# Scaling of an mLSTM chunk's values cut in halves and moved, with four small moves around it, in a fused mLSTM and MLP kernel

## The chip, the cores and the metric

The kernel runs on one core of one Trainium2 chip, in one launch. The metric is the device time of a whole execution in microseconds (us). The kernel before was run five times: 469.13, 469.29, 468.72, 469.12 and 468.61 us, median 469.12. All runs had a granted TensorE clock of 1.0 of full speed.

The engines are named as the profile names them: PE is TensorE (matmuls), PEld its weight loads, DVE is VectorE, ACT is ScalarE, POOL is GpSimd and SP is SyncE, which here does nothing but issue DMAs.

## The reference

The first half is an mLSTM cell with B=4 batches, H=8 heads, S=768 tokens and head size D=40, the second an MLP with a quick GELU on the 3072 tokens x 320 values that the cell gives.

```python
for t in range(S):
    m_new = np.maximum(f_gate[:, :, t] + m, i_gate[:, :, t])
    f_stab = np.exp(f_gate[:, :, t] + m - m_new)
    i_stab = np.exp(i_gate[:, :, t] - m_new)
    m = m_new
    C = f_stab[..., None, None] * C + i_stab[..., None, None] * einsum('bhd,bhe->bhde', v_t, k_t)
    n = f_stab[..., None] * n + i_stab[..., None] * k_t
    h_tilde = einsum('bhde,bhe->bhd', C, q_t)
    denom = np.maximum(np.abs(einsum('bhd,bhd->bh', n, q_t)), 1.0)
    y[:, :, t] = sigmoid(o_t) * h_tilde / denom
x = y.transpose(0, 2, 1, 3).reshape(3072, 320)
h = x @ w_in                                   # 320 x 2048
out = (h * sigmoid(1.702 * h)) @ w_out         # 2048 x 320
```

The inputs of the cell are float32. `moe_w_in` and `moe_w_out` are float64 in memory, and the kernel reads them as pairs of 32-bit words.

## The kernel before, in words

**Tiling.** The 768 tokens are cut into NW=6 chunks w of 128. In each chunk the recurrence is worked out as a masked matrix product within the chunk (scores, weights, values) plus what the state of the chunks before gives. The 32 pairs of batch and head go by batch b (8 heads) in chunk 0, and by halves c (16 heads, two batches) in later chunks. Then the chunk's 512 tokens (4 batches x 128) go through the MLP in 8 pairs of 128 hidden columns (`up`, later `up_fast`, which saves multiplications by Strassen's scheme) and through `w_out` (`down`, `down_fast`). While PE works at the MLP of chunk w, the cell of chunk w+1 is done in between.

**Converting the weights.** The float64 words are turned into float32 in 20 pieces of 128 x 512. Pieces 0 to 9 are `w_in`: 0, 1, 3, 4, 5, 6, 8, 9 go into `w_in_sb` (two halves c of the first 256 rows, by 512 columns), 2 and 7 into `w_in_x` (the last 64 rows). Pieces 10 to 19 are `w_out`. Each piece takes six instructions:

```python
242  A.activation(out=dst, in_=hi.bitcast(FP), func=AF.Abs)              # convert_high
246  A.activation(out=lo, in_=lo, func=AF.Copy, scale=2.0 ** -29)        # convert_low
255  V.tensor_scalar(out=dst, in0=dst, scalar1=HI_MIN, scalar2=HI_MAX, op0=OP.max, op1=OP.min)
256  V.tensor_scalar(out=dst_u, in0=dst_u, scalar1=3, ...)               # convert_mid, as 255 and 258
258  V.scalar_tensor_tensor(out=dst_u, in0=hi, scalar=0xC0000000, ...)
264  V.tensor_tensor(out=dst_u, in0=dst_u, in1=lo, op=OP.add)            # convert_add
```

The first two are on ScalarE, the others on VectorE. Where the profile names a piece by its target, piece 0 is `w_in_sb` at L264 before 26 us, piece 1 the next `w_in_sb`, piece 2 the first `w_in_x`.

**What sets the order.** The schedule is manual: each engine runs its instructions in the order in which the program issues them, and waits by semaphores for the other engines' results. So a call's place in the program is its place on each engine's queue. Tiles come from pools with a fixed number of buffers; PSUM has two pairs of banks (`ps_a`, tag "a": `p_t`, `p_cols`, `p_x`, `p_o`, `p_i`, `p_c`, `p_s` in turn) and four single banks (`ps_m`). A tile that takes a buffer waits until the readers of its last tenant are done. Nearly all DMAs are issued by SP, one after the other; each chunk's gates go out to DRAM and come back as columns and rows: `m_row` (L298), `st_row` and `d_row` (L322) are written by `gates`, `columns_in` (L340 to 347) reads `raw` back, and `spread` (L391 to 398) reads `m_row` into `wt`, spread over the partitions. In the program `spread(1)` stands at j=4 of chunk 0, behind `load(1, "v")` and `columns_in(1)`.

**The start and chunk 0** (L821 to 864). PE begins with 18 matmuls of 128 columns on a tile of zeros (L197) that no one reads. Then, per batch b, come the transposes of k and q (L371), the weights of the chunk (`weights`, L411 to 426: matmuls into PSUM and two exponentials on ScalarE), the scores (L436 to 445), and for b of 2 and 3 the values of batch b-2 (`values`, L478 to 489) with `outputs` (L458 to 476). `outputs` forms `y` on VectorE and, in chunk 0, ends with a tail copy of 64 columns on GpSimd (L476). `seam` (L520) transposes a batch's `y` into `xT`, the MLP's input: three transposes, the third of which reads the tail copy, and copies out of PSUM on ScalarE, but for the last batch, whose first copy is on VectorE (L528). Between the third and the fourth seam stand `columns(0)` (L354: one transpose `p_cols` and one Exp that turn the gates' sums into `cols`), the first half of the conversion of piece 1, and `keep_busy(1, spare, 7)` (L189 to 193), one matmul of 512 and seven of 32 columns that nobody reads. Pieces 1 and 2 are converted behind the last seam.

**The MLP of chunk 0** (L880 to 900). For even j, `up` does two pairs of columns: L608 multiplies `w_in_sb`, L614 `w_in_x`. The pieces of weights that later j need are converted ahead of and inside these calls (`converted`, L866): pieces 3 and 4 ahead of the first `up`, piece 5 inside it. In the same loop `scale(0, 0)`, `carry(0, 0)`, `scale(0, 1)`, `carry(0, 1)` follow `up` at j = 0, 1, 2, 3. `scale` (L570 to 574) is one GpSimd instruction that multiplies 16 heads of `v_st` (128 partitions x 656 values) by an exponential in `cols`, into `vw`; `carry` (L576) multiplies `k` by `vw` on PE and copies the sum into the state. GpSimd needs nothing from PE for both scalings, so it runs them one behind the other.

```python
891  (carry if j % 2 else scale)(0, j // 2)       # for j < B
```

Later, `weights(1, 0)` has ScalarE do 32 exponentials on `wt` (L429) when the rows are there and GpSimd the mask (L433), `scores(1, c)` multiplies them with the scores on VectorE (L456), and `values(1, 0)` multiplies `wt` with `v_st` into `p_o` (L497) and the queries with the state into `p_i` (L505). Pieces 17 to 19 are converted during `down` (L934).

Of the kernel before, what the change touches and what calls it, by code (L numbers as in the profile page):

```python
# [8 lines left out]
FP = mybir.dt.float32  # L9
# [3 lines left out]
OP = mybir.AluOpType  # L13
# [4 lines left out]
L = 128  # L18
# [8 lines left out]
def kernel(  # L27
# [13 lines left out]
    B, H, S, D = q.shape  # L41
    BH = B * H
    DM = H * D
# [4 lines left out]
    D1 = D + 1  # L48
# [5 lines left out]
    PH = 2 * H  # L54
# [3 lines left out]
    const = ctx.enter_context(tc.tile_pool(name="const", bufs=1))  # L58
# [134 lines left out]
            T.matmul(bank[:, 0:32], idle, idle[:, 0:32], start=True, stop=True)  # L193

    p_idle = ps_m.tile([128, W], FP, tag="m", name="p_idle")
    for _ in range(18):
        T.matmul(p_idle[:, 0:128], idle, idle, start=True, stop=True)  # L197
    ident = const.tile([128, 128], FP, name="ident")
    make_identity(nc, ident)
    make_identity(nc, ident_b)  # L200
# [17 lines left out]
    for t in (k_0, q_st):  # L218
        G.memset(t[:, :, D:DP], 0.0)

    state = [const.tile([128, BH // 2, D1], FP, name=f"state{i}") for i in range(2)]
    state_mid = const.tile([128, BH // 2, D1], FP, name="state_mid")

# [20 lines left out]
    def convert_low(n):  # L244
        lo, hi, dst = words(n)
        A.activation(out=lo, in_=lo, func=AF.Copy, scale=2.0 ** -29)
# [211 lines left out]
    def outputs(w, hs, u):  # L458

        n = hs.stop - hs.start  # L460
        c, b = divmod(hs.start // H, 2)
        den = work.tile([L, n, 1], FP, tag="den", name="den")
        V.tensor_scalar(out=den, in0=u[:, :, D:D1], scalar1=-1.0, scalar2=1.0, op0=OP.mult, op1=OP.max)
        V.tensor_tensor(out=den, in0=u[:, :, D:D1], in1=den, op=OP.max)
        V.reciprocal(out=den, in_=den)
        z = eo[w][:, hs, :]
        V.scalar_tensor_tensor(out=z, in0=z, scalar=1.0, in1=u[:, :, 0:D], op0=OP.add, op1=OP.mult)
        if b == 0:
            ys[w, c] = work.tile([L, 2, DM + 64], FP, tag="y", name="y")
        for x in range(n // H):  # L470
            y, h = ys[w, c][:, b + x], slice(hs.start + x * H, hs.start + x * H + H)
            V.scalar_tensor_tensor(out=y[:, 0:DM].rearrange("p (h d) -> p h d", d=D), in0=eo[w][:, h, :], scalar=0.5,
                                   in1=den[:, x * H:(x + 1) * H].to_broadcast([L, H, D]), op0=OP.mult, op1=OP.mult)
        if w == 0:
            y = ys[w, c][:, b:b + n // H]
            G.tensor_copy(out=y[:, :, DM:DM + 64], in_=y[:, :, DM - 64:DM])  # L476

    def values(w, c):  # L478
        if w == 0:
            hs = slice(c * H, (c + 1) * H)  # L480
            po = ps_m.tile([L, H, D1], FP, tag="m", name="p_o")
            for p in range(NP):
                for i in range(2):
                    h = 2 * p + i
                    for x in range(2):
                        t = slice(x * HL, x * HL + HL)
                        T.matmul(po[t, h, :], wt[w, c][:, p, i, t], v_st[:, c * H + h, :], start=True, stop=True)  # L487
            outputs(w, hs, po)
            return
        hs = slice(c * PH, (c + 1) * PH)  # L490
        po, pi = banks("p_o"), banks("p_i")

        for j in range(NJ):
            for i in range(2):
                for x in range(2):
                    t, r = slice(x * HL, x * HL + HL), slot(i, x)
                    T.matmul(po[t, i, j * D1:(j + 1) * D1], wt[w, c][r, j, i, :], v_st[r, c * PH + 2 * j + i, :],  # L497
                             start=True, stop=True)
        for j in range(NJ):
            b, p = 2 * c + j // NP, j % NP  # L500
            for i in range(2):
                r = slice(i * 64, i * 64 + D)
                for x, s in enumerate((state[w % 2], state_mid)):
                    t = slice(x * HL, x * HL + HL)
                    T.matmul(pi[t, i, j * D1:(j + 1) * D1], qT[w, b][r, p, t], s[r, c * NJ + j, :], start=True,  # L505
                             stop=True)
        u = work.tile([L, PH, D1], FP, tag="u", name="u")
        v = u.rearrange("s (j i) d -> s i j d", i=2)
        g = cols[w][:, BH + c * PH:BH + (c + 1) * PH].rearrange("s (j i) -> s i j", i=2).unsqueeze(3)
        view = lambda z: z[:, :, 0:NJ * D1].rearrange("s i (j d) -> s i j d", d=D1)  # L510
        V.tensor_tensor(out=v, in0=view(pi), in1=g.to_broadcast([L, 2, NJ, D1]), op=OP.mult)
        V.tensor_tensor(out=v, in0=view(po), in1=v, op=OP.add)
        outputs(w, hs, u)

    def x_of(w):
# [51 lines left out]
        engine.tensor_tensor(out=dst[:, js], in0=old[:, js], in1=d.unsqueeze(2).to_broadcast([128, NJ, D1]),  # L567
                             op=OP.mult)

    def scale(w, c):  # L570
        hs = slice(c * PH, (c + 1) * PH)
        vw[w, c] = work.tile([L, PH, D1], FP, tag="u", name="vw")
        e = cols[w][:, 2 * BH + c * PH:2 * BH + (c + 1) * PH].unsqueeze(2).to_broadcast([L, PH, D1])
        G.tensor_tensor(out=vw[w, c], in0=v_st[:, hs, :], in1=e, op=OP.mult)  # L574

    def carry(w, c):  # L576
        js = slice(c * NJ, (c + 1) * NJ)
# [255 lines left out]
    for b in range(B):  # L833
        if b >= 2:
            transposes(0, b)
            open_first(b - 2)
            values(0, b - 2)
        weights(0, b)
        if b == 0:
            convert_high(0)  # L840
            transposes(0, 1)
        scores(0, b)
        if b == 0:
            convert_mid(0)
        if b == 1:
            convert_low(0)
            convert_add(0)
    load_gates(1)
# [5 lines left out]
    values(0, 3)  # L854
    seam(0, 0, 1)
    seam(0, 1, 0)
    columns(0)
    convert_high(1)
    spare = ps_m.tile([128, W], FP, tag="m", name="p_idle")
    keep_busy(1, spare, 7)  # L860
    seam(0, 1, 1)
    convert_low(1)
    convert_end(1)
# [16 lines left out]
    for w in range(NW):  # L880
        more = w + 1 < NW
        if w == 0:
            for j in range(NF // 2):
                if j % 2 == 0:
                    ahead, behind = converted[j // 2]
                    run([(convert, p) for p in ahead] + [(fetch, p) for p in fetched.get(j // 2, ())])
                    up(w, j, lambda: run([(convert, p) for p in behind]))
                if j == 6:
                    load(1, "o")
                if j < B:  # L890
                    (carry if j % 2 else scale)(0, j // 2)
                if j == 3:
                    masks()
                    gates(1)
                if j == 4:
                    load(1, "v")
                    columns_in(1)
                    spread(1)
                if j >= B:
                    transposes(1, j - B)  # L900
        else:
            token_sums(w)
            if more:
                gates(w + 1)
                load(w + 1, "o")
            for j in range(NF // 2):
                up_fast(w, j)
                if w == 1 and j < 4:
                    weight_sums(j)
                if more and j == 2:  # L910
                    load(w + 1, "vk")
                    columns_in(w + 1)
                    spread(w + 1)
                if more and j:
                    for n in ((), (0, 2), (4,), (6, 1), (3,), (5, 7), ())[j - 1]:
                        block_transposes(w + 1, n)
                if more and j == 7:
                    columns_turn(w + 1)
                if 2 <= j < 6:
                    hidden_difference(w, j - 2)  # L920
                if j >= 6:
                    hidden_sums(w, (j - 6,), G)
            gelu_fast(w, NF // 2 - 1)
            hidden_sums(w, (2, 3), V)
        side = attention(w + 1) if more else {}
        if w == 0:
            columns_turn(1)

            blocks = [(lambda b=b, n=n: down(w, b, n)) for n0 in (0, 2) for b in range(B) for n in (n0, n0 + 1)]
        else:  # L930
            blocks = down_fast(w, 0) + down_fast(w, 1)
        for i, block in enumerate(blocks):
            if w == 0 and i in (0, 4, 5):
                convert((17, 18, 19)[max(i - 3, 0)])  # L934
            if w + 2 < NW and i == (6 if w == 0 else 0):
                load_gates(w + 2)
            if w + 2 < NW and i == 13:
                load_squares(w + 2, "kq" if w else "k")
            if w == 0 and i == 15:
                load_squares(w + 2, "q")  # L940
            block()
            run(side.get(i, []))
            if w == 0 and i in (11, 13):
                input_sums(slice(0, 4) if i == 11 else slice(4, 8))
# [30 lines left out]
```

## Time and profile before

| | |
|---|---|
| median of five runs | 469.12 us |
| the profiled execution's own time | 469.13 us |
| its span in the profile | 467.4 us |
| PE busy | 462.1 us, 99% of the span, 5063 matmuls |
| PEld busy | 388.2 us, 83% |
| DVE busy | 341.9 us, 73% |
| ACT busy | 189.7 us, 41% |
| POOL busy | 156.8 us, 34% |
| DMA traffic | 52.21 MB, a mean of 112 GB/s |

By stage, from the table of windows (DMA is the share of the 16 DMA engines):

| stretch, us | what PE does | length | PE busy | DMA |
|---|---|---|---|---|
| 0 to 26 | chunk 0 of the cell | 26 | 24.55 | 0.93 |
| 26 to 33 | last seam, first `up` | 7 | 6.17 | 1.07 |
| 33 to 70 | `up` of chunk 0 | 37 | 37.00 | 0.97 |
| 70 to 94.4 | `down`, cell of chunk 1 | 24.4 | 24.40 | 0.55 |
| 94.4 to 116 | `down`, cell of chunk 1 | 21.6 | 21.60 | 0.55 |
| 116 to 467 | chunks 1 to 5 | 351 | 348.41 | 0.51 |

How to read it: the profile is one execution, recorded on the chip; its own time (469.13) is 1.7 us longer than the span between the first and the last recorded instruction. A line of the timeline gives the start, the duration, the engine, the program line, the operation with output and inputs, the sizes and a count of instructions that stand together; a bracket at the end is the idle time of that engine just before, with the engine, tile and line that ended it. SPq lines are DMA issues on SP's queue. Busy time on PE is the time that matmuls are in it; the table says where PE waits (stretches whose busy time is less than their length), not whether a matmul could be shorter.

### The profile page before, as it was taken

The page shows a single profiled execution, that of the slowest core. Times are in us where ns is not written, and L with a number is a line of the kernel's source. Part 1 is how long each engine was busy: PE and PEld are TensorE (multiplying, and loading weights), DVE is VectorE, ACT ScalarE, POOL GpSimd, SP SyncE. Part 2 cuts the span into 40 slices and gives each one's busy share as a digit, 9 for nine tenths or more (in the row PEclk, how much of TensorE's full clock was granted, in tenths as well). Part 3 has the DMA queues.
Part 4 walks back from the last instruction along what each step waited for, and adds up shares of the span by engine and source line. Part 5 has one row for each costly group of instructions (what it writes and reads, how often), then busy time and mean ns, then how long its engine had stood idle before and what let it go on. Part 6 is the DMA issues. An engine that isn't in the chain of part 4 may idle for free.

```text
span 467.4 us, 12343 instructions
## 1 busy us (share of the span) xinstructions
PE 462.1 (99%) x5063; PEld 388.2 (83%) x5063; DVE 341.9 (73%) x698; ACT 189.7 (41%) x431; POOL 156.8 (34%) x142
## 2 busy tenths in 40 slices
PE   8999999999999999999999999999999999999997
PEld 6867777777778999678999767999878999876997
DVE  5787998789788976688875778887768866544612
ACT  5676776500536700554800453900454820264100
POOL 5020004300798700266700257610158620157100
PEclk9999999999999999999999999999999999999999
DMA  8999979228994025999024998115999305000000
GB/s 164 194 272 166 292 134 219 30 54 193 181 146 111 3 72 132 192 125 162 6 60 111 196 148 149 23 36 122 177 140 124 88 18 140 29 1 0 1 29 29
DMA packets 138393, 52.21 MB, mean 112 GB/s; under 512 B 106976, under 2 KB 134496, under 8 KB 138336
## 3 DMA queue, kind: packets, MB, share of 16 engines
q1 hardware_dynamic: 130288, 49.76, 55.8%
q10 hardware_dynamic: 8048, 1.66, 1.8%
q8 instruction: 40, 0.66, 0.6%
q14 instruction: 17, 0.14, 0.1%
HBM read 43.86 MB, written 7.54 MB: 110 GB/s over the span
## 4 chain that ended last, share of the span: by engine, by line
PE 97%; DVE 1%; ACT 0%; issue 0%; DVEq 0%
PE p_out L796 33%; PE p_h L687 27%; PE p_h L695 8%; PE p_out L742 8%; PE p_h L608 5%; PE p_c L584 3%; PE p_o L497 2%; PE p_s L453 2%; PE p_i L505 2%; PE p_t L380 2%; PE p_h L614 2%; PE p_s L442 1%; PE p_o L487 1%; PE p_w L409 1%; PE p_idle L197 0%; PE p_x L525 0%
## 5 line engine op out<-in xcount | busy, mean ns | idle before, releaser
L733 POOL TENSOR_TENSOR g<-g,parts 128x512 f32<-128x512 f32 x30 | 38.3, 1276 | 188.1 <-DVE parts L725 181.0
L721 ACT COPY parts<-p_h 128x256 f32<-128x256 f32 x40 | 15.0, 374 | 148.6 <-PE p_h L687 145.0
L796 PE MATMUL p_out<-w_out_sb,g 128*128 128x160 f32 x480 | 69.5, 301 | 0.0
L796 PEld LDWEIGHTS p_out<-w_out_sb,g 128*128 128x128 f32 x480 | 66.5, 190 | 0.9
L687 PE MATMUL p_h<-xT,w_in_sb 128*128 128x256 f32 x240 | 66.9, 388 | 0.0
L668 ACT ACTIVATE g<-g 128x512 f32<-128x512 f32 x80 | 50.1, 631 | 39.3 <-DVE g L728 24.6
L687 PEld LDWEIGHTS p_h<-xT,w_in_sb 128*128 128x128 f32 x240 | 43.7, 190 | 18.5 <-issue 6.7
L801 DVE TENSOR_TENSOR o_sb<-o_sb,p_out 128x160 f32<-128x160 f32 x70 | 21.4, 318 | 40.9 <-PE p_out L796 40.3
L796 PE MATMUL p_out<-t_sb,s 128*128 128x160 f32 x320 | 47.1, 300 | 0.0
L724 DVE TENSOR_TENSOR t_x<-p_h,parts 128x256 f32<-128x256 f32 x40 | 16.8, 419 | 38.9 <-PE p_h L695 34.5
L796 PEld LDWEIGHTS p_out<-t_sb,s 128*128 128x128 f32 x320 | 44.4, 190 | 0.2
L687 PE MATMUL p_h<-t_x,s_in 128*128 128x256 f32 x160 | 41.1, 379 | 0.0
L429 ACT ACTIVATE wt<-wt,cols 128x64 f32<-128x64 f32 x160 | 38.8, 334 | 2.9 <-DMA wt<-m_row 2.8
L695 PE MATMUL p_h<-xT,w_in_x 64*128 64x512 f32 (+1 forms) x192 | 39.8, 540 | 0.0
L574 POOL TENSOR_TENSOR vw<-v_st,cols 128x656 f32<-128x656 f32 x12 | 17.0, 1439 | 61.5 <-ACT cols L362 61.5
L742 PE MATMUL p_out<-w_out_sb,g 128*128 128x320 f32 x128 | 35.7, 436 | 0.0
L687 PEld LDWEIGHTS p_h<-t_x,s_in 128*128 128x128 f32 x160 | 30.4, 190 | 4.2
L742 PEld LDWEIGHTS p_out<-w_out_sb,g 128*128 128x128 f32 x128 | 23.9, 190 | 9.6
L608 PE MATMUL p_h<-xT,w_in_sb 128*128 128x256 f32 x128 | 30.0, 386 | 0.5 <-DVE w_in_sb L264 0.5
L725 DVE TENSOR_TENSOR parts<-p_h,t_x 128x512 f32<-128x512 f32 x40 | 27.7, 692 | 3.5
L732 ACT COPY g<-p_h 128x512 f32<-128x512 f32 x30 | 17.4, 581 | 30.3 <-PE p_h L695 25.0
L608 PEld LDWEIGHTS p_h<-xT,w_in_sb 128*128 128x128 f32 x128 | 23.5, 190 | 7.1 <-issue 3.0
(192 smaller groups left out, 842.6 us busy)
## 6 DMA issues: line engine op xcount, KB each, us to landing
wt<-m_row SPq DMA_DIRECT2D x20, 256.0 KB, 5.1
k_sq<-in_k_dram SPq DMA_DIRECT2D x16, 320.0 KB, 6.1
q_sq<-in_q_dram SPq DMA_DIRECT2D x16, 320.0 KB, 10.3
out_dram<-o_sb SPq DMA_DIRECT2D x24, 160.0 KB, 2.0
eo<-in_o_gate_dram SPq DMA_DIRECT2D x5, 640.0 KB, 8.0
bits<-in_moe_w_in_dram SPq DMA_DIRECT2D x6, 512.0 KB, 10.6
q_sq<-x_row SPq DMA_DIRECT2D x10, 256.0 KB, 3.0
v_st<-in_v_dram SPq DMA_DIRECT2D x14, 160.0 KB, 5.6
```

What stands on the lines that cost most here:

```text
L429: A.activation(out=x[:, h, :], in_=x[:, h, :], func=AF.Exp, scale=-1.0, bias=cols[w][:, c * PH + h:c * PH + h + 1])
L574: G.tensor_tensor(out=vw[w, c], in0=v_st[:, hs, :], in1=e, op=OP.mult)
L608: T.matmul(ph[j][i][:, t], w_in_sb[:, c, f * 128:(f + 1) * 128], x[:, c, t], start=(first and c == 0 and n == 0), stop=(not first and c == ...
L668: A.activation(out=gs[w, j][:, i, :], in_=gs[w, j][:, i, :], func=AF.Gelu_apprx_sigmoid)
L687: T.matmul(out, a, x[n], start=start, stop=stop)
L695: T.matmul(row[:, t], w_in_x[r, j, :], rest_x[r, 2, t], start=(not late and h == 0), stop=(late and h == n - 1))
L725: V.tensor_tensor(out=y[:, half_w:3 * half_w].rearrange("p (a t) -> p a t", a=2), in0=flat[:, half_w:3 * half_w].rearrange("p (a t) -> p a ...
L732: A.copy(out=g[:, 0, :], in_=row0)
L733: G.tensor_tensor(out=g0, in0=g0, in1=u, op=OP.add)
L742: T.matmul(po, gs[w, f // 2][:, f % 2, b * L:(b + 1) * L], w_out_sb[:, f, :], start=(f == 0), stop=(f == NF - 1))
L796: T.matmul(po, a(f), b[:, f, :], start=(f == 0), stop=(f == NH - 1))
L801: V.tensor_tensor(out=dst, in0=x, in1=po, op=OP.add)
```

## The change

It makes six edits.

1. The matmuls on zeros at the start (L197) become 25 of 96 columns.
2. `columns(0)` moves from behind the third seam to behind `scores(0, 1)`, ahead of the second half of the conversion of piece 0.
3. `scale(0, 0)` is cut into two halves of 8 heads, one batch each, which follow `values(0, 0)` and `values(0, 1)` in the loop over batches.
4. The tail copy of `y` (L476) of the last batch goes to VectorE.
5. `keep_busy(1, spare, 7)` loses its seven short matmuls.
6. `scale(0, 1)` moves to j = 1, ahead of `carry(0, 0)`, and a new function, `wait_for`, stands ahead of it: a one-column copy on GpSimd from the target of piece 4 into a new tile `mark`. GpSimd runs it only when piece 4 is converted, and the scaling behind it.

The new tile takes a place in the constant pool ahead of the states, and all tiles that are laid out behind it lie 32 bytes further. The order of SP's DMA issues is unchanged.

```diff
     p_idle = ps_m.tile([128, W], FP, tag="m", name="p_idle")
-    for _ in range(18):
-        T.matmul(p_idle[:, 0:128], idle, idle, start=True, stop=True)
+    for _ in range(25):
+        T.matmul(p_idle[:, 0:96], idle, idle[:, 0:96], start=True, stop=True)
...
+    mark = const.tile([L, 1], FP, name="mark")
     state = [const.tile([128, BH // 2, D1], FP, name=f"state{i}") for i in range(2)]
...
-            G.tensor_copy(out=y[:, :, DM:DM + 64], in_=y[:, :, DM - 64:DM])
+            (V if hs.stop == BH else G).tensor_copy(out=y[:, :, DM:DM + 64], in_=y[:, :, DM - 64:DM])
...
-    def scale(w, c):
-        hs = slice(c * PH, (c + 1) * PH)
-        vw[w, c] = work.tile([L, PH, D1], FP, tag="u", name="vw")
-        e = cols[w][:, 2 * BH + c * PH:2 * BH + (c + 1) * PH].unsqueeze(2).to_broadcast([L, PH, D1])
-        G.tensor_tensor(out=vw[w, c], in0=v_st[:, hs, :], in1=e, op=OP.mult)
+    def scale(w, c, part=0, parts=1):
+        n = PH // parts
+        hs = slice(c * PH + part * n, c * PH + (part + 1) * n)
+        if part == 0:
+            vw[w, c] = work.tile([L, PH, D1], FP, tag="u", name="vw")
+        e = cols[w][:, 2 * BH + hs.start:2 * BH + hs.stop].unsqueeze(2).to_broadcast([L, n, D1])
+        G.tensor_tensor(out=vw[w, c][:, part * n:(part + 1) * n], in0=v_st[:, hs, :], in1=e, op=OP.mult)
+
+    def wait_for(x):
+
+        G.tensor_copy(out=mark, in_=x[:, 0:1])
...
             values(0, b - 2)
+            scale(0, 0, b - 2, 2)
...
         if b == 1:
+            columns(0)
             convert_low(0)
             convert_add(0)
...
     seam(0, 1, 0)
-    columns(0)
     convert_high(1)
     spare = ps_m.tile([128, W], FP, tag="m", name="p_idle")
-    keep_busy(1, spare, 7)
+    keep_busy(1, spare)
...
-                if j < B:
-                    (carry if j % 2 else scale)(0, j // 2)
+                if j == 1:
+                    wait_for(w_in_sb[:, 1, 512:1024])
+                    scale(0, 1)
+                if j < B and j % 2:
+                    carry(0, j // 2)
```

## The prediction

> **What bounds the kernel now.** I read the page first: PE is busy 99% of the span and 97% of the chain of work that ended last, so a change pays only where PE waits, or where something that PE will meet next comes earlier too. Then I looked for PE's waits with the timeline of PE from 25 to 34 us. They are two, both for VectorE's conversion of `w_in`:
>
> ```profile
> 26.08 3.84 PE L608 MATMUL p_h<-xT,w_in_sb 128*128 128x256 f32 x16
> 30.38 1.99 PE L608 MATMUL p_h<-xT,w_in_sb 128*128 128x256 f32 x8 [0.47 <-DVE w_in_sb L264]
> 32.74 1.99 PE L614 MATMUL p_h<-xT,w_in_x 64*128 64x512 f32 x8 [0.36 <-DVE w_in_x L264]
> ```
>
> The square bracket is idle time and who ended it. The timelines of VectorE and then of GpSimd for the same stretch tell why VectorE is late:
>
> ```profile
> 26.28 0.29 DVE L528 COPY xT<-p_x 128x128 f32<-128x128 f32 x1 [0.77 <-PE p_x L525]
> 26.49 0.85 DVE L255 TENSOR_SCALAR w_in_sb<-w_in_sb 128x512 f32<-128x512 f32 x1
> 27.38 1.40 DVE L256 TENSOR_SCALAR w_in_sb<-w_in_sb 128x512 uint32<-128x512 uint32 x1
> ...
> 30.25 0.42 DVE L255 TENSOR_SCALAR w_in_x<-w_in_x 128x512 f32<-128x512 f32 x1
> 30.70 0.43 DVE L256 TENSOR_SCALAR w_in_x<-w_in_x 128x512 uint32<-128x512 uint32 x1
> ```
>
> ```profile
> 25.77 2.72 POOL L574 TENSOR_TENSOR vw<-v_st,cols 128x656 f32<-128x656 f32 x2
> ```
>
> L255 and L256 of piece 1 take 0.85 and 1.40 us beside the two scalings (25.77 to 28.49), the same lines of piece 2 take 0.42 and 0.43 with GpSimd idle. So the scalings cost VectorE 0.43 + 0.97 = 1.40 us on the way to PE.
>
> The third question is what PE meets afterwards. In the trace PE has no idle time from 34 to 116 us, but one of its waits is nearly due. The timelines of ScalarE, VectorE and PE around 77 to 95 us show it:
>
> ```profile
> 77.59 7.75 ACT L429 ACTIVATE wt<-wt,cols 128x64 f32<-128x64 f32 x32 [2.79 <-DMA wt<-m_row]
> 85.24 0.66 ACT L242 ACTIVATE w_out_sb<-bits 128x512 f32<-128x512 f32 x1
> ```
>
> ```profile
> 85.93 0.90 DVE L255 TENSOR_SCALAR w_out_sb<-w_out_sb 128x512 f32<-128x512 f32 x1 [2.32 <-ACT w_out_sb L242]
> ...
> 91.32 0.69 DVE L264 CUSTOM_DVE_ANT_0 w_out_sb<-bits,w_out_sb 128x1024 uint16<-128x1024 uint16 x1
> 91.93 2.35 DVE L456 TENSOR_TENSOR wt<-p_s,wt 128x1024 f32<-128x1024 f32 x2
> ```
>
> ```profile
> 93.47 1.14 PE L497 MATMUL p_o<-v_st,wt 64*64 64x41 f32 x64
> 94.42 0.23 PE L505 MATMUL p_i<-state,qT 40*64 40x41 f32 x1
> ```
>
> ScalarE's 32 exponentials of the next chunk start at 77.59, when the rows of `wt` land by DMA. Behind them ScalarE begins piece 18, VectorE converts pieces 18 and 19 without a gap from 85.93, and then multiplies the scores (L456, 91.93 + 2.35 = 94.28). PE's p_i needs the PSUM pair that the second L456 frees. It starts at 94.42, 0.14 after that; where a wait binds, PE starts 0.05 behind its producer (26.57 to 26.63, 30.33 to 30.38, 32.68 to 32.74). So PE is only **0.09 us** later than this other chain.
>
> Does that other chain move with the change? Its head is the landing of `wt`, issued by SP at 70.56 to 72.95:
>
> ```profile
> 61.15 6.43 SPq L120 DMA_DIRECT2D v_st<-in_v_dram x3
> 68.08 1.91 SPq L345 DMA_DIRECT2D raw<-st_row x4
> 70.04 0.47 SPq L347 DMA_DIRECT2D raw<-d_row x1
> 70.56 2.39 SPq L397 DMA_DIRECT2D wt<-m_row x4
> ```
>
> From 17.8 to 73 us SP issues without a pause, or waits for the landing of a transfer issued some eight before (landed 57.46, next issue 57.52; 58.67 and 58.69). The stage view gives the 16 DMA engines a share of 1.07 from 26 to 33 us and 0.97 from 33 to 70. The nearest engine event that an issue before `wt` names is m_run (L291, done 50.49), 7.0 us ahead of its issue at 57.52. The view of SP's waits puts 5.8 us on DVE L264 of `w_in_x` (the issue at 40.85 that ends at 46.61). I don't take that as a cause: the built program has this issue wait for the add of piece 0, done at 14.76; the end at 46.59 is a neighbour in time, and the queue was moving 160-byte packets. So I hold the landing at 77.51 fixed.
>
> **The change, part by part** (against the profiled execution's 469.13 us).
>
> *Start.* 18 matmuls of 128 columns stand 0.107 apart (1.06 to 2.95, 1.92 us); 25 of 96 at the same rate take 25 x 0.080 = 2.00: +0.08. PE is then ordered behind them until 25 us (its waits up to 7.86 for ScalarE's copies follow from its own transposes).
> [...] Here the spacing falls from 0.107 to 0.056 at 6.8 us. [...]
>
> *Columns behind the second scores.* p_cols takes 0.14 of PE (25.10 to 25.24), now at 12.1 us where PE has no idle time. The next transposes now wait for the second exponential of batch 1 (ends 12.16, PE arrives at 12.2): at most 0.1. Together +0.14 to +0.25. ScalarE's Exp (0.20) goes ahead of L246 at 12.04; that is needed by VectorE at 14.08, and would end near 13.3. The two buffers of the PSUM pair then change hands so that p_cols no longer waits for xT at 25.10 (0.22 idle) and the last p_x waits for the second xT copy, not the third.
>
> *Short matmuls dropped, tail copy on VectorE.* The last p_x started at 25.66, 0.15 behind y (25.51), held by the 7 short matmuls; now 0.05 behind it: -0.10. Its third transpose needs the tail copy: 0.24 on GpSimd; on VectorE I take the same as the upper end, so it is ready 0.34 behind y, when that transpose would come anyway (0.05 + 0.19 + 0.12 = 0.36): nothing.
> Sum so far: VectorE's L528 comes at +0.08 + 0.17 - 0.10 = about 0.15 later.
>
> *Halves of the first scaling.* 2.72/2 = 1.36 us for 656 elements, so about 0.7 for each half, behind the tail copies at 16.22 and 20.40. GpSimd is idle there for 3.9 and 3.5 us, so the tail copies queued behind are not late. VectorE beside it runs L444, with one operand in PSUM; the nearest row, L456 of that kind, takes 1.22 us with and without GpSimd busy: nothing. If cover failed, up to 0.7 each.
>
> *Conversion of piece 1 free.* VectorE saves 1.40, so the add of piece 2 ends at 32.68 - 1.40 = 31.28 (+0.15). PE's first pass ends at 29.54 + 0.22 = 29.76; 8 records of 0.216 follow at once, to 31.48; the step from L608 to L614 takes 0.09 more (40.98 to 41.29). L614 starts at 31.58 (+0.15) instead of 32.74, and no longer waits. **PE's lead: 1.16 - 0.15 = 1.0 us.**
>
> *Second scaling behind piece 4.* The mark copy (0.10 to 0.24, by the 1-column memsets and the tail copies) and 1.36 us of scaling now start near 36.1 and meet L255 and L256 of piece 5: up to 1.40 on VectorE there. PE needs piece 5 at 47.92 less 1.0, its add ended at 39.75, and VectorE was idle for 2.04 before 44.14: hidden, 7 us in reserve. `vw` of that half is needed at 46.86; done near 38.
>
> *What takes the place of the wait.* The lead of 1.0 reaches p_o and p_i. p_o needs the first L456 (93.15), p_i the second (94.28): p_i starts at 94.33, not at 93.4. **Gain kept: 94.42 - 94.33 = 0.09 us**; some 0.9 us is waited for there. All later work hangs on p_i. 469.13 - 0.09 = 469.04.
>
> The five runs span 468.61 to 469.29. Two chains of nearly one length decide each run, and one of them loses 1 us; so the median should lie somewhat lower than the profiled case moves, toward the fast runs. I take **468.9**.
>
> **Rivals.**
> *The lead is kept* (0.18): `wt` lands earlier, because SP does hang on an early engine event or transfers run better. The wait view's 5.8 us on L264 speaks for it, the program's semaphore against it. The 20 `wt` transfers land 4.1 to 7.1 us after issue, the deciding one takes 6.4, so there is room for all of it: 469.13 - 1.0 = 468.1.
> *`wt` lands later* (0.10): slower. Tiles allocated behind `mark` lie 32 bytes further, the DMA engines are at 0.9, and the landing alone now sets the time. From 0.09 us late on, each bit counts; the longest of the 20 would give 7.1 - 6.4 - 0.09 = +0.6: 469.7.
> *It doesn't free VectorE* (0.05): GpSimd is pushed late and the scaling still meets piece 1; the waits at 30 us stay and the added 0.15 is hidden by nothing: 469.3.
>
> **How the numbers follow.** Likeliest 468.9 (0.67, own range 468.4 to 469.4). The range goes down to the kept lead, 468.1, less 0.2 for what the five runs of before scatter about their middle, and up to most of the late landing, 469.6. A measurement here tells about 0.2% (0.94 us) from no change: faster means under 468.2, slower over 470.1. The kept lead reaches the first, mostly: 0.15. The late landing hardly reaches the second: 0.03. Same: 0.82.
>
> **What would show it.** L255 and L256 of piece 1 at 0.42 and 0.43; no idle before PE's L608 and L614 near 30 us; L614 near 31.7; the two long rows at piece 5 instead; `wt` exponentials still at 77.5 to 77.7 with more idle before them; a new PE wait before L497 or L505 on DVE L456, together 0.8 to 1.0 us. Wrong if the exponentials start before 77, or if PE reaches p_i without waiting.

## The result and the profile after

The changed kernel takes **467.91 us** (median of 23 runs, 467.26 to 468.49). The kernel before, run beside it, takes 468.83 us (43 runs, 468.39 to 469.38). The ratio is 0.998 with a 95% interval of 0.9974 to 0.9985: faster by 0.92 us. The forecast was 468.9, some 0.2 below the 469.12 from which the prediction started; what came true is the rival that had 0.18, the lead is kept (468.1).

The profiled execution after took 467.26 us (span 465.5) against 469.13 (467.4). These two differ by 1.87 us, twice as much as the medians. The timeline of PE around 30 us, in the profile after (start, duration, engine, line, operation; the changed kernel's lines are 1 to 7 further on):

```profile
24.87 0.59 PE L526 MATMUL p_x<-ident,y 128*128 128x128 f32 x3 [0.57 <-DVE y L473]
25.29 5.62 PE L615 MATMUL p_h<-xT,w_in_sb 128*128 128x256 f32 x24
30.85 1.99 PE L621 MATMUL p_h<-xT,w_in_x 64*128 64x512 f32 x8
```

Both brackets of before (0.47 and 0.36) are gone, the 24 matmuls stand in one row, and from the first of them to L621 it takes 5.56 us instead of 6.66 (26.08 to 32.74). The timelines of VectorE and of GpSimd say why:

```profile
25.49 0.29 DVE L529 COPY xT<-p_x 128x128 f32<-128x128 f32 x1 [0.54 <-PE p_x L526]
25.70 0.42 DVE L256 TENSOR_SCALAR w_in_sb<-w_in_sb 128x512 f32<-128x512 f32 x1
26.15 0.43 DVE L257 TENSOR_SCALAR w_in_sb<-w_in_sb 128x512 uint32<-128x512 uint32 x1
...
35.11 0.42 DVE L256 TENSOR_SCALAR w_in_sb<-w_in_sb 128x512 f32<-128x512 f32 x1
35.57 1.53 DVE L257 TENSOR_SCALAR w_in_sb<-w_in_sb 128x512 uint32<-128x512 uint32 x1
```

```profile
15.43 0.74 POOL L577 TENSOR_TENSOR vw<-v_st,cols 128x328 f32<-128x328 f32 x1
...
19.80 0.73 POOL L577 TENSOR_TENSOR vw<-v_st,cols 128x328 f32<-128x328 f32 x1
...
35.26 0.32 POOL L581 COPY mark<-w_in_sb 128x1 f32<-128x1 f32 x1 [11.66 <-DVE w_in_sb L265]
35.53 1.29 POOL L577 TENSOR_TENSOR vw<-v_st,cols 128x656 f32<-128x656 f32 x1
```

Piece 1 is converted at full speed, the halves lie at 15 and 20 us, and the long row has moved to piece 5 (1.53), where nothing waits for it. The prediction expected the lead to end at p_i. The timelines of ScalarE, VectorE and PE there:

```profile
73.40 7.75 ACT L430 ACTIVATE wt<-wt,cols 128x64 f32<-128x64 f32 x32 [0.49 <-DMA wt<-m_row]
```

```profile
87.75 2.35 DVE L457 TENSOR_TENSOR wt<-p_s,wt 128x1024 f32<-128x1024 f32 x2
```

```profile
91.58 1.14 PE L498 MATMUL p_o<-v_st,wt 64*64 64x41 f32 x64
92.53 0.23 PE L506 MATMUL p_i<-state,qT 40*64 40x41 f32 x1
```

The exponentials start at 73.40, not at 77.59; the scores are ready at 90.10, 2.43 us ahead of p_i. PE waits for nothing here.

### The profile page after: what moved, and what is told of

Its sections match the earlier page's. It is cut to its first block, busy times and chain, and to the rows that moved or that the text cites. A ratio compares the mean times of both kernels' runs of the same rounds, so it can differ in the third digit from the quotient of the medians.

```text
span 465.5 us, 12346 instructions
## 1 busy us (share of the span) xinstructions
PE 460.5 (99%) x5063; PEld 387.1 (83%) x5063; DVE 340.4 (73%) x699; ACT 189.7 (41%) x431; POOL 156.9 (34%) x143
## 4 chain that ended last, share of the span: by engine, by line
PE 97%; DVE 1%; DMA 0%; issue 0%; DVEq 0%
PE p_out L803 33%; PE p_h L694 27%; PE p_h L702 8%; PE p_out L749 8%; PE p_h L615 6%; PE p_c L591 3%; PE p_o L498 2%; PE p_s L454 2%; PE p_i L506 2%; PE p_h L621 2%; PE p_t L381 1%; PE p_s L443 1%; PE p_o L488 0%; PE p_w L422 0%; DMA fi<-in_f_gate_dram 0%; PE p_w L424 0%
## 5 line engine op out<-in xcount | busy, mean ns | idle before, releaser
L694 PEld LDWEIGHTS p_h<-xT,w_in_sb 128*128 128x128 f32 x240 | 43.7, 190 | 18.5 <-issue 6.7
L577 POOL TENSOR_TENSOR vw<-v_st,cols 128x656 f32<-128x656 f32 (+1 forms) x13 | 17.1, 1328 | 51.3 <-DMA wt<-m_row 35.8
L615 PE MATMUL p_h<-xT,w_in_sb 128*128 128x256 f32 x128 | 29.8, 385 | 0.0
L702 PEld LDWEIGHTS p_h<-xT,w_in_x 64*128 64x128 f32 x192 | 16.9, 186 | 14.7 <-issue 13.5
```

What stands on the lines that cost most here:

```text
L577: G.tensor_tensor(out=vw[w, c][:, part * n:(part + 1) * n], in0=v_st[:, hs, :], in1=e, op=OP.mult)
L615: T.matmul(ph[j][i][:, t], w_in_sb[:, c, f * 128:(f + 1) * 128], x[:, c, t], start=(first and c == 0 and n == 0), stop=(not first and c == ...
L694: T.matmul(out, a, x[n], start=start, stop=stop)
L702: T.matmul(row[:, t], w_in_x[r, j, :], rest_x[r, 2, t], start=(not late and h == 0), stop=(late and h == n - 1))
```

## The experiments

Theory A: the lead of PE is kept, because the landing of chunk 1's rows is not fixed at 77.51 but differs from execution to execution, and mostly leaves room. Theory B: the lead is lost at p_i, as predicted, and the gain comes from the start and the small edits. Theory C, a special case: the rows come earlier because the tiles behind `mark` lie elsewhere.

**The moved scalings alone, and the rest alone.** `scalings_alone` is before with these edits (and with `mark`, `wait_for` and the parts of `scale` that they use):

```diff
             values(0, b - 2)
+            scale(0, 0, b - 2, 2)
...
         if b == 1:
+            columns(0)
...
-    columns(0)
...
+                if j == 1:
+                    wait_for(w_in_sb[:, 1, 512:1024])
+                    scale(0, 1)
```

> Before, with the halves of the first scaling, the second scaling behind piece 4, and the columns turned behind the second scores (they need them); the start, the short matmuls and the tail copy stay as before. Theory A (the lead of PE that the free conversion gives is kept to the end, about 1.0 us by the prediction's own sum): 467.9 +- 0.2, against 468.8 for before. Theory B (the gain of the change comes from the start and the small edits, the lead being lost at p_i): 468.7. In the profile, by A, p_i (L506 of the changed kernel) starts without a wait for VectorE.

Measured 467.74 (7 runs; before 468.72), ratio 0.9974 (0.9963 to 0.9984). A second time, beside the changed kernel:

> The kernel with the scalings and the columns moved alone, once more, to set it beside the changed kernel on one chip. If the other three edits (start, tail copy, short matmuls) are worth nothing: within 0.15 of the changed kernel. The prediction's sum for them was +0.08 for the start and -0.10 for the short matmuls.

> The changed kernel once more, beside the three of this group. 467.9. From the first matmul of p_s to the first of the pair L621 it should take 22.9 us again (23.85 before), and from there to the end 434.7 unless PE waits at p_o or p_i.

467.97 (12 runs), ratio 0.9982 (0.9973 to 0.999), against 468.04 (8 runs), ratio 0.9978 (0.9968 to 0.9987). So the whole gain is in the scalings with the columns that they need, and the other three edits are worth nothing that can be measured. The stage from p_s to L621 was 22.91 us in `after_again` (9.10 to 32.01), and 434.68 from there to the end.

`rest_alone` is before with the other edits: the start, the columns, the tail copy, the dropped short matmuls.

> Before with the 25 matmuls of 96 columns, the columns behind the second scores, the tail copy on VectorE and without the short matmuls; both scalings stay at their places of before. Theory A: no gain, 468.8 to 469.0 (the prediction's sum was +0.15 for these edits); the two waits near 30 us stay. Theory B: 467.9 to 468.1.

469.42 (12 runs, 468.88 to 471.17), ratio 1.0022 (1.001 to 1.0034): slower, worse than either theory said. The columns are ready early here, so GpSimd begins both scalings right behind the third tail copy, and now meets the last output. Timelines of GpSimd, VectorE and PE of this kernel:

```profile
24.04 2.78 POOL L575 TENSOR_TENSOR vw<-v_st,cols 128x656 f32<-128x656 f32 x2
```

```profile
24.71 0.96 DVE L473 SCALAR_TENSOR_TENSOR y<-eo,den 128x320 f32<-128x320 f32 x1
25.71 1.16 DVE L477 COPY y<-y 128x64 f32<-128x64 f32 x1
```

```profile
25.82 0.47 PE L526 MATMUL p_x<-ident,y 128*128 128x128 f32 x2 [1.04 <-DVE y L473]
26.92 0.33 PE L526 MATMUL p_x<-ident,y 128*128 128x128 f32 x1 [0.63 <-DVE y L477]
27.09 7.31 PE L609 MATMUL p_h<-xT,w_in_sb 128*128 128x256 f32 x24
```

y takes 0.96 instead of 0.49, the tail copy 1.16 instead of 0.20, and PE is idle for 1.67 us. The row of 24 matmuls then takes 7.31 us instead of 5.62, though nothing interrupts it. The table of windows gives the reason (stretch, length, busy time and count of PE, PEld, DVE, ACT and POOL, granted clock, DMA share, GB/s):

```profile
27.00:29.00 2.00, 1.96 (x8) 1.35 (x9) 1.64 (x4) 1.39 (x3) 0.00 (x0) 0.83 1.01 401
29.00:31.00 2.00, 2.00 (x6) 1.62 (x5) 1.80 (x5) 2.00 (x5) 0.00 (x0) 0.50 1.08 239
31.00:33.00 2.00, 2.00 (x9) 1.66 (x9) 1.83 (x4) 1.98 (x3) 0.00 (x0) 0.81 1.14 226
```

The clock was halved (0.50 from 29 to 31 us). By the trace's own record this lasted from 28.34 to 31.75, 3.41 us, and cost 1.7 (7.31 less 5.62). Five of the twelve runs lie at 470.78 to 471.17, the others at 468.88 to 469.44. The mean granted clock recorded for each run parts the same two groups: it is 0.996 in each of the five and 0.999 to 1.0 in the seven, and 3.41 us at half clock in a span of 469.1 make 1 - 1.71/469.1 = 0.996. By this estimate a stretch of half clock comes in these five executions only. That the idle time on PE brings it is the author's estimate and isn't shown: one execution was profiled. The seven others have a median of 469.23, still 0.5 above before.

**Halves alone.** `scalings_alone` without `wait_for`, and with `scale(0, 1)` at j = 2 as before:

```diff
-                if j == 1:
-                    wait_for(w_in_sb[:, 1, 512:1024])
-                    scale(0, 1)
+                if j == 2:
+                    scale(0, 1)
```

> Before with the columns behind the second scores and the first scaling in halves between the outputs; the second scaling stays where before has it, so GpSimd runs it right behind the last tail copy, some 1.36 us long, and it still meets L255 of piece 1 and the start of L256. Of the 1.40 us that VectorE lost to both, 0.5 to 0.8 should be left, so 0.4 to 0.7 of the gain of 0.9 is there: 468.1 to 468.5, with L256 of piece 1 shorter than 1.40.

467.98 (11 runs; before 469.03), ratio 0.9984 (0.9975 to 0.9993): nearly all of the gain, more than expected. Timelines of GpSimd, VectorE and PE:

```profile
25.52 1.29 POOL L577 TENSOR_TENSOR vw<-v_st,cols 128x656 f32<-128x656 f32 x1
```

```profile
26.24 0.85 DVE L256 TENSOR_SCALAR w_in_sb<-w_in_sb 128x512 f32<-128x512 f32 x1
27.12 0.43 DVE L257 TENSOR_SCALAR w_in_sb<-w_in_sb 128x512 uint32<-128x512 uint32 x1
```

```profile
25.83 5.62 PE L615 MATMUL p_h<-xT,w_in_sb 128*128 128x256 f32 x24
31.52 1.99 PE L621 MATMUL p_h<-xT,w_in_x 64*128 64x512 f32 x8
```

The scaling that remains still holds up one VectorE instruction (0.85, as before), but not the second (0.43 instead of 1.40). VectorE keeps 0.97 of the 1.40, and PE needs no more: from L615 to L621 it takes 5.69 us against 5.56. The rows show that the lengthened instruction ends at 27.09, 0.28 behind the end of the scaling (26.81), a little less than the 0.42 that it takes alone, and that the scaling lengthens one instruction, not all beside it: L529 takes 0.29 beside this one, as in the profile after, where GpSimd is idle then. Why the two hold each other up isn't shown.

**Is the landing held up by the kernel?** `after_pad64` has a wider `mark`, so that the tiles behind it have before's remainder by 64 bytes; `before_mark` is before with the tile added and not used.

```diff
-    mark = const.tile([L, 1], FP, name="mark")
+    mark = const.tile([L, 16], FP, name="mark")
```

> The changed kernel with a mark tile of 16 columns in place of 1, so that the tiles behind it lie 64 bytes further than before instead of 32, with the same remainder by 64 as before. Theory C (the rows of wt land 4 us earlier in the profile after because the tiles behind mark lie on multiples of 64 bytes now): wt lands about as in before, 77 us or later, less what SP's chain gained by the start, p_i waits again, and the time is 468.6 to 468.8. Theory A (the chain of transfers differs from execution to execution, not by the tiles' places): 467.9, like the changed kernel.

> The kernel before with nothing but the new tile mark, which nobody reads or writes: all tiles behind it lie 32 bytes further, as in the changed kernel. Theory C: the rows of wt land some 2 to 4 us earlier than 77.5, time unchanged or up to 0.1 less (p_i had waited for 0.09 in the profile of before). Theory A: nothing moves but by chance, 468.8; wt may land anywhere in a few us about 75.

> The same kernel as the one with the mark of 16 columns, once more, for a second profile and more runs. Theory C (the places of the tiles make the rows of wt late): the second row transfer lands at 76 or later again. Theory A: it lands anywhere from 73 to 78, and the time is 467.9 again.

`before_mark`: 468.89 (12 runs; before 468.72), ratio 1.0003 (0.9995 to 1.0012). `after_pad64`: 467.89 and 467.96 (11 runs each), ratios 0.998 (0.9972 to 0.9989) and 0.9982 (0.9974 to 0.9991). Where the tiles lie moves no median: theory C falls. The first profile of `after_pad64`, however, is an execution in which the prediction came true, 468.73 us and the slowest of its eleven. Timelines of ScalarE, VectorE and PE:

```profile
77.23 7.75 ACT L430 ACTIVATE wt<-wt,cols 128x64 f32<-128x64 f32 x32 [3.89 <-DMA wt<-m_row]
```

```profile
91.58 2.35 DVE L457 TENSOR_TENSOR wt<-p_s,wt 128x1024 f32<-128x1024 f32 x2
```

```profile
92.85 1.24 PE L498 MATMUL p_o<-v_st,wt 64*64 64x41 f32 x64 [0.93 <-DVE wt L457]
93.98 0.25 PE L506 MATMUL p_i<-state,qT 40*64 40x41 f32 x1
```

Here the rows land at 77.14, PE waits 0.93 before p_o and reaches the end 435.90 us after L621 (31.12 to 467.01) instead of 434.69: the lead is lost, 1.2 us in all. In the second profile of the same kernel they land at 76.24 and p_i comes 0.11 behind the scores, without a wait (434.69). So the step that the prediction described exists; it isn't what most executions meet. Of the seven profiled executions of the changed kernel, `scalings_alone`, `halves_alone` and `after_pad64`, this one waits; in two others p_i comes only 0.33 (`halves_alone`) and 0.11 behind the scores, in the other four 2.32 to 2.76.

Two more profiled executions of the kernel before:

> The kernel before, one more profiled execution. The prediction held the landing of the second row transfer at 77.51. If that is how this kernel runs: within 0.5 of 77.5, and p_i about 0.1 behind the second multiplication of scores. Theory A (the landing differs by execution): earlier, as in eight of the eleven other kernels' profiles, and p_i 1 to 3 us behind it.

> The same as the look before it: the landing within 0.5 of 77.5 if the kernel sets it, anywhere from 73 to 78 if the execution does.

The rows landed at 73.47 and 74.25. The first of the two (469.16 us) by ScalarE, VectorE, PE and SP's queue:

```profile
74.83 7.75 ACT L429 ACTIVATE wt<-wt,cols 128x64 f32<-128x64 f32 x32
```

```profile
89.18 2.35 DVE L456 TENSOR_TENSOR wt<-p_s,wt 128x1024 f32<-128x1024 f32 x2
```

```profile
94.44 0.23 PE L505 MATMUL p_i<-state,qT 40*64 40x41 f32 x1
```

```profile
54.87 0.64 SPq L299 DMA_DIRECT2D m_row<-m_run  x1
67.96 2.38 SPq L397 DMA_DIRECT2D wt<-m_row  x4
```

PE is at p_i at 94.44, as in the first profile (94.42), but the scores were ready 2.92 us earlier instead of 0.14. From 26 us on PE and VectorE ran alike in the two executions (first `up` at 26.08 and 26.11): VectorE's add of piece 7, on which the view of SP's waits puts 5.8 us, starts at 45.90 in both, and its L291, which makes m_run, at 50.02 in both. SP nevertheless issued `m_row` 2.65 us earlier (54.87 instead of 57.52). So neither of these events of VectorE set when the rows came. The profile that the prediction worked from had the latest landing of all those with the rows at this place in the queue; nothing in that one trace shows it.

**Is the lead lost further on?** Five more matmuls on zeros behind the last seam:

```diff
     seam(0, 1, 1)
+    keep_busy(5, spare)
```

> The changed kernel with five more matmuls of 512 columns on zeros (0.216 us each by the spacing in the profile) behind the last seam, ahead of the first matmul of the MLP: PE comes 1.08 us later to the rest. Theory A (nothing holds PE behind them, the lead is kept): +1.0 to 1.1, 468.9 to 469.0, about the time of before, and the wait for the rows rarer than in the changed kernel. The prediction's reason (the lead is lost at p_i): 467.9 to 468.1, no dearer.

468.71 (11 runs), ratio to before 0.9992 (0.9984 to 1.0001), against 468.04 and 467.91 for the changed kernel: 0.67 to 0.80 more, far from nothing. In its profile p_s to L621 takes 24.03 us, 1.1 more than in the changed kernel, and the rest 434.67. Why the medians show less than 1.1 isn't settled; runs of one kernel scatter over 1 us.

**Rows later, rows earlier, scores earlier.**

```diff
                 if j == 6:
+                    spread(1)
                     load(1, "o")
...
                     columns_in(1)
-                    spread(1)
```

> The changed kernel with the rows of wt for chunk 1 fetched behind pieces 18 and 19 instead of ahead of them. Its second transfer should land some 4 to 5 us later, where the transfers of pieces 18 and 19 landed (76.7 to 79.2 in the profile after), so the 32 exponentials start near 78 instead of 73.4, the second multiplication of scores ends near 95 instead of 90.1, and PE, which is at p_o at 91.6, waits. If the chain from the rows to p_o is what would bind next (theory A and the prediction alike): p_o with 1.5 to 3 us of idle time before it, time 469.2 to 471. If PE could wait there without cost, or the chain is elsewhere: 467.9.

472.69 (12 runs, 467.97 to 476.45); the ratio to before over the eight runs up to 474.58 is 1.004 (1.0013 to 1.0067), some 1.9 us. That the later fetch costs time is shown, and 1.9 more than before, 470.7, lies in the expected range. The wait expected isn't shown: the profiled execution was a lucky one (468.91) with rows at 77.32, exponentials at 77.40 and 0.27 of waiting at p_o. The granted clock of the runs tells of a second cost: it is 1.0 in the five up to 469.85, 0.996 at 472.08, 0.993 and 0.992 at 474.58 and 473.3, and 0.989 in the four above 476, as one, two and three stretches of half clock would make it (an estimate from the 3.41 us of `rest_alone`: 0.996, 0.993 and 0.989). What PE waited for in these runs was not profiled.

```diff
-                    load(1, "v")
                     columns_in(1)
                     spread(1)
+                    load(1, "v")
```

> The changed kernel with the columns and rows of chunk 1 fetched ahead of its values v instead of behind them. The rows land near 68 to 70, so the exponentials start when the columns are there, near 74 or earlier, in every execution. Theory A (the rows' landing differs by some us from execution to execution and delays PE only in the latest of them): median 467.7 to 467.9, and the slowest runs (468.3 to 468.5 for the changed kernel) less slow by up to 0.5. If the pin holds a good part of the lead in most runs: 467.3 or less.

469.72 (12 runs, 468.1 to 473.88), ratio 1.0031 (1.0011 to 1.005): a miss, since the expectation forgot who else needs v. The rows landed at 70.09, but chunk 1's scalings multiply v. Timelines of PE and GpSimd:

```profile
78.59 2.39 PE L591 MATMUL p_c<-vw,t_sb 64*64 64x41 f32 x128 [1.18 <-POOL vw L577]
```

```profile
77.25 2.53 POOL L577 TENSOR_TENSOR vw<-v_st,cols 128x656 f32<-128x656 f32 x2 [39.48 <-ACT wt L430]
```

GpSimd starts them at 77.25 (72.61 in the profile after), and PE waits 1.18 for them. The bracket names an exponential of `wt`, which these scalings don't read; the last part of v, which they read, landed at 77.09 (67.97 in the profile after). The four slowest of the twelve (471.05 to 473.88) have a granted clock of 0.996 to 0.992, the others 0.999 or 1.0.

```diff
-            if w == 0 and i in (0, 4, 5):
-                convert((17, 18, 19)[max(i - 3, 0)])
+            if w == 0 and i in (0, 4, 7):
+                convert((17, 18, 19)[min(i // 3, 2)])
```

> The changed kernel with piece 19 converted behind the scores of chunk 1 instead of ahead of them, so that the second multiplication of scores ends 2.35 us earlier whenever the rows are late. If late rows cost the changed kernel something in a part of its runs: median 467.7 to 467.9, the slowest runs below 468.3 (468.5 to 469.05 so far). If they cost it much in most: 467.2 or less. If piece 19 comes late for down: a wait of PE before L749 near 95 us, and up to 1 us more.

468.04 (11 runs, 467.34 to 468.54), ratio 0.9978 (0.9969 to 0.9987), the median of the changed kernel beside it. Its rows landed at 76.51, and p_i was still 1.90 behind the scores. Without the 2.35 us that the edit gives, the scores of this execution would by this sum have come 0.45 too late, so it is one more in which the rows are late. The room gained is not needed in the median: late rows cost the changed kernel little.

**The start alone:**

> Before with the 25 matmuls of 96 columns at the start and nothing else. Prediction: +0.08 at most, so 468.7 to 468.9. Theory B's remainder (the start brings the full clock earlier): 468.0 to 468.4. The moment of the full clock should lie anywhere from about 4 to 7.5 us in either kernel.

468.75 (11 runs; before 468.83), ratio 0.9998 (0.9989 to 1.0007): nothing.

## Why the prediction was wrong, point by point

Three spans, read from PE's starts in each profile, account for the result (the last column is the landing of the second row transfer, on which the exponentials wait):

| kernel | p_s to first `up` | first `up` to `w_in_x` | `w_in_x` to end | rows land |
|---|---|---|---|---|
| before | 17.20 | 6.66 | 434.67 | 77.51 |
| before, 2nd execution | 17.96 | 6.65 | 434.69 | 73.47 |
| before, 3rd execution | 17.20 | 6.65 | 434.77 | 74.25 |
| changed | 17.38 | 5.55 | 434.69 | 73.31 |
| changed, again | 17.36 | 5.55 | 434.68 | 74.56 |
| `scalings_alone` | 17.35 | 5.56 | 434.68 | 73.42 |
| `halves_alone` | 17.36 | 5.69 | 434.72 | 76.10 |
| `after_pad64` | 17.35 | 5.56 | 435.90 | 77.14 |

-1.10 in the second column and +0.16 in the first give -0.94; the medians moved by -0.92. The first column isn't quite steady: the 17.96 holds 0.69 us of PE's waiting for ScalarE's copy of `qT`, which the other executions of before don't have.

- *Conversion freed*: right. L255 and L256 of piece 1 went from 0.85 and 1.40 to 0.42 and 0.43, VectorE saves 1.40, and PE 1.10 of the 1.16 that was forecast.
- *Columns*: right, 0.14 to 0.25 forecast, 0.16 found. Halves at 0.7: right (0.74 and 0.73; they are nearly or quite over when VectorE's L445 begins at 16.02 and 20.62, so what they would cost it isn't shown). *Second scaling hidden*: right, 1.53 for one row at piece 5, nobody waits (the mark copy took 0.32, more than the 0.10 to 0.24 that was taken for it).
- *Short matmuls*: wrong, -0.10 forecast. The last p_x starts 0.15 behind y in both profiles (25.51 to 25.66, 24.72 to 24.87), so the short matmuls had not held it. *Start*: +0.08 forecast, nothing measurable. *Tail copy*: 0.20 on VectorE, hidden, right.
- *Lead*: 1.0 forecast, 0.94 found.
- **The step that failed** is "So I hold the landing at 77.51 fixed", and with it the gain kept of 0.09. The reason given was that SP waits for no engine from 17.8 us on. For the two events that it weighed the second execution of before bears it out, but that did not make the landing fixed. In before itself the rows landed at 73.47 and 74.25 as well, with 2.92 and 2.74 us of room at p_i instead of 0.14: the room was there without the change, and the lead of 0.94 fits into it. In the profile after, both signs of being wrong that the prediction named are there: the exponentials start before 77, and PE reaches p_i without waiting. Over the profiles of these kernels with the rows' place in the queue unchanged the landing lies between 73.06 and 77.51. The one profile that was read was the latest of them, and the 0.14 us beside p_i was its chance. In `after_pad64` a like landing makes the predicted wait.
- *Reading toward the fast runs* because two chains of nearly one length decide each run: it rested on the same step.

Why the transfers differ by 4 us between executions of one kernel is open. Between the first two executions of before (77.51 and 73.47) 2.65 us of the difference stand when `m_row` is issued (57.52 and 54.87), so they come from the transfers ahead of it. Another 1.43 arise in the second row transfer itself, which takes 6.43 us from issue to landing in the one (71.08 to 77.51) and 5.00 in the other (68.47 to 73.47).

## What to carry to other kernels

A slack beside a DMA in one profile is a sample, not a bound (at p_i it was 0.14 us in one execution of before, 2.92 and 2.74 in two others): before calling a saved wait "pinned" by a transfer, profile the same kernel again. Here two more executions of before would have been enough. Where GpSimd and VectorE meet, ask which VectorE instruction a GpSimd instruction holds up (here two scalings one each, 0.85 and 1.40 us instead of 0.42 and 0.43), and whether it stands on the way to PE; moving one half of the GpSimd work out of the way brought nearly all the gain (ratio 0.9984, against 0.998 for the changed kernel). And an instruction that is made ready earlier has to be followed to where it will now run: with the columns early and the scalings left alone, the kernel became slower (469.42 against 468.72).

## What the runs showed of the hardware

Between executions of one kernel the full clock came at different moments: by the traces' clock records at 6.80, 4.01 and 3.72 us in three executions of before, at 4.09 and 6.92 in two of the changed kernel. The timelines of PE show it in the transposes, here before and then after:

```profile
3.90 1.09 PE L380 MATMUL p_t<-ident,k_sq 128*128 128x128 f32 x4
```

```profile
3.88 0.71 PE L381 MATMUL p_t<-ident,k_sq 128*128 128x128 f32 x4
```

The two profiled executions of the changed kernel took 467.26 and 468.40, with L621 at 30.85 and 32.01. So up to about 1 us of a profiled execution's time is the start's chance, which is why the two profiles first compared, where p_s starts at 8.89 and 7.91, differ by 1.87 us and the medians by 0.92. In the record of `rest_alone` the full clock came at 4.45 us, was lost at 28.34 and came back at 31.75.

The 1.67 us of idle time on PE there, in two parts, were followed by a half clock that cost 1.7 us more, as much as the wait itself. In the runs recorded here a granted clock below 0.999 occurs in three kernels alone, `rest_alone`, `after_late_rows` and `after_early_rows`, all of them slower than before. Whether a wait brings it, and how long a one, isn't shown: in the profiled executions the 1.67 us of `rest_alone` came with it, the 1.18 us of `after_early_rows` and the 0.93 us of `after_pad64` did not (granted clock 1.0 in both).
